# A fused attention-and-gating kernel: another order of the work inside a step, the spatial weight transposed later, and the last two batches finished together

## The chip, the cores and the metric

The kernel runs on one core of a Trainium2 chip. The metric is the device time of one launch in microseconds (us). The core's engines are TensorE (PE in the profile, its weight loads PEld), VectorE (DVE), ScalarE (ACT) and GpSimd (POOL); SyncE (SP) and POOL issue the DMAs. Each engine takes its instructions in the order of its own list, and a semaphore makes it wait for another engine where data or a buffer is still missing.

## The reference

Two layers in a row. The first is linear attention with learned features, for 8 batches, 8 heads, 576 tokens, head size 64 and 128 features:

```python
def phi(x):
    proj = np.einsum('bhsd,df->bhsf', x, w_phi)
    proj = proj - np.max(np.abs(proj), axis=-1, keepdims=True)
    return np.concatenate([np.exp(proj), np.exp(-proj)], axis=-1)
q_p, k_p = (phi(q), phi(k))
kv = np.einsum('bhsf,bhsd->bhfd', k_p, v)
z = np.sum(k_p, axis=2)
num = np.einsum('bhsf,bhfd->bhsd', q_p, kv)
den = np.einsum('bhsf,bhf->bhs', q_p, z)[..., None] + 1e-06
x = num / den                          # then heads side by side: 576 tokens x 512
```

The second is a gated layer in which tokens are mixed by a 576 x 576 matrix:

```python
h = np.maximum(x @ w_in, 0.0)          # 512 -> 1024
u, v = h[..., :512], h[..., 512:]
v_n = (v - mean(v)) / sqrt(var(v) + 1e-06)
v_s = np.einsum('ts,bsd->btd', w_spatial, v_n) + b_spatial[None, :, None]
out = (u * v_s) @ w_out                # 512 -> 512
```

## The kernel before

A batch has 576 tokens, which is four blocks of 128 and a rest of 64, called the tail. Tails of two neighbouring batches share one 128-row tile, and the two batches make a group: four groups of two batches.

**Stage A, attention, runs in steps over 36 units.** A unit is a pair of heads of one batch (four units a batch, its 512 tokens of the four blocks) or the tail of a group (all eight heads, two batches' tails). Each unit passes through a pipeline of five steps. In step `i` the kernel does, for unit `i`, the key projection (`a_keys`: matmuls L233, maxima on DVE L245, exponentials on ACT L248), the scaling of the values by the key maxima (`a_scale`: ACT L260, POOL L265 to L277), the query projection and its maxima (`a_queries`: L233, L254) and the split of the query maxima into two bfloat16 parts (`a_split`: L284 and L285). For unit `i+1` it transposes k and q (`a_transpose`, L224, copies to `kT` on ACT L227 and to `qT` on DVE L228); from batch 3 on the DMA engines deliver the transposed data, issued on SP. For unit `i-1` it transposes the maxima (`a_max_t`, L289, L290). For unit `i-2` it sums keys times values (`a_kv`, L330 and L332, copy to `kv` on ACT L334) and makes the query features (`a_qfeat`, L300 and L304, exponentials on ACT L317). For unit `i-3` it multiplies the two and divides (`a_num`, L349, L339, L340), and for unit `i-4` it transposes the quotient into `xT` (`a_x_t`, L358, L359). The order in which these parts are written inside `step` (L557) is the order in which every engine meets them.

**Stage B, the gated layer, is a queue of tasks.** When the last unit of a batch is in `xT`, `b_tasks` (L523) appends the batch's tasks: `b_v` (v half of the first product, L393, relu on ACT L395, statistics on DVE L396 and L397), `b_ln` (root and normalization on POOL, L403 to L410), `b_u` (u half, L446, L448), `b_s` (mixing by the transposed spatial weight `w_spT`, L467 and L468, gating on DVE L470) and `b_o` (output product L490, copy on ACT L492 into `ob`, DMA L498 on SP), and for the tail the same with the ending `_tail`. The function `fill` (L550) runs between the parts of a step: it adds a share of `RATE` to a credit and takes tasks from the queue as long as the credit covers half of the first task's cost. Four calls with a share of 0.25 each stand in a step; the credit is cut at `RATE / 2`. What is left in the queue after the last step runs at the end without stage A beside it.

**Tails.** For groups in `SPLIT` (L516), which are the first and the last, each batch does its own tail, so its mixing and its output follow its own u half. For the other groups only the second batch of the group holds the tail's tasks, and it runs the mixing and the output for both batches.

**The spatial weight** is transposed on PE (`transpose_spatial`, L192 to L202, copies on DVE L196 and L203): three of its five parts after step 4 and two after step 5. All products and transposes of the kernel use one pool of eight PSUM banks (L57). The output tile `ob` has four buffers. `EARLY = 7` (L165) makes the first seven units' splits run on DVE, later ones on POOL.

Of the kernel before, what the change touches and what calls it, by code (L numbers as in the profile page):

```python
# [16 lines left out]
def kernel(  # L17
# [22 lines left out]
    P = 128  # L40
# [123 lines left out]
    NM = 3  # L164
    EARLY = 7  # L165
    mhl, mT = [], []
# [44 lines left out]
    def a_transpose(u):  # L211
        src = st[u["b"]] if u["pair"] else gs[u["g"]]
        if "kT" in src:
            for x in ("kT", "qT"):
                u[x] = src[x][:, 4 * u["pj"]:4 * u["pj"] + 4, :] if u["pair"] else src[x]
            return
        pt = psum.tile([P, 2, 4, P], BF16, tag="bank", name="pt")
        for i, x in enumerate((src["k"], src["q"])):
            for j in range(4):
                if u["pair"]:  # L220
                    blk = x[:, 2 * u["pj"] + j // 2, (j % 2) * P:(j % 2 + 1) * P]
                else:
                    blk = x[:, 2 * j:2 * j + 2, :]
                nc.tensor.transpose(out=pt[:, i, j, :], in_=blk, identity=ident)  # L224
        u["kT"] = a1.tile([P, 4, P], BF16, tag="kT", name="kT")
        u["qT"] = a1.tile([P, 4, P], BF16, tag="qT", name="qT", bufs=4)
        nc.scalar.copy(out=u["kT"], in_=pt[:, 0])  # L227
        nc.vector.tensor_copy(out=u["qT"], in_=pt[:, 1])  # L228

# [90 lines left out]
    def a_kv(u):  # L320
# [5 lines left out]
        for hh in range(2):  # L326
            h = 2 * u["pj"] + hh
            for s in range(2):
                for c in range(NB):
# [3 lines left out]
                                 rhs=dg["vs"][:, bl, s, h, :], start=False, stop=True)  # L333
        nc.scalar.copy(out=d["kv"][:, 2 * u["pj"]:2 * u["pj"] + 2, :, :], in_=pv)  # L334

# [17 lines left out]
    def a_x_t(u):  # L353
        if u["pj"] == 0:
            st[u["b"]]["xT"] = s2.tile([P, KC, T0], BF16, tag="xT", name="xT", bufs=3)
        pt = psum.tile([P, NB, P], BF16, tag="bank", name="pt")
        for pos in range(NB):
            nc.tensor.transpose(out=pt[:, pos, :], in_=u["x"][:, pos].rearrange("p h d -> p (h d)"), identity=ident)  # L358
        nc.vector.tensor_copy(out=st[u["b"]]["xT"][:, u["pj"], :], in_=pt.rearrange("p n t -> p (n t)"))  # L359

# [147 lines left out]
    for g in range(G):  # L508
        units.append(dict(pair=False, g=g, i=len(units)))
# [3 lines left out]
    units[0], units[1] = units[1], units[0]  # L513
    units[0]["i"], units[1]["i"] = 0, 1
    NU = len(units)
    SPLIT = (0, G - 1)  # L516

    def unit(i):
        return units[i] if 0 <= i < NU else None
# [3 lines left out]
    def b_tasks(b):  # L523
# [22 lines left out]

    RATE = 3.4
    credit = [0.0]

    def fill(share):  # L550
        credit[0] = min(credit[0] + RATE * share, RATE / 2)
        while queue and credit[0] >= queue[0][0] / 2:
            cost, task = queue.pop(0)
            task()
            credit[0] -= cost

    def step(i):  # L557
# [3 lines left out]
        if u:  # L561
            a_keys(u)
            a_scale(u)
        fill(0.25)
        if z and z["pair"]:
            a_kv(z)
        if u:
            a_queries(u)
            a_split(u)
        fill(0.25)  # L570
        if n:
            a_transpose(n)
        if w:
            a_max_t(w)
        fill(0.25)
        if x and x["pair"]:
            a_x_t(x)
            if x["pj"] == NP - 1:
                g, bl = x["g"], x["b"] % 2
                alone = g in SPLIT  # L580
                if alone or bl == 1:
                    tail_x_t(g, [bl] if alone else [0, 1])
                queue.extend(b_tasks(x["b"]))
        if z:
            a_qfeat(z)
        fill(0.25)
        if y and y["pair"]:
            a_num(y)
            if y["pj"] == NP - 1:
                g, bl = y["g"], y["b"] % 2  # L590
                alone = g in SPLIT
                if alone or bl == 1:
                    tail_num(g, [bl] if alone else [0, 1])

    for i in range(NU + 4):
# [47 lines left out]
```

## Time and profile before

| what | value |
|---|---|
| runs | 315.26, 314.56, 315.25 us; median 315.25 us |
| profiled execution | 313.68 us, span 311.9 us |
| busy share of the span | PE 87%, DVE 69%, ACT 73%, POOL 59% |
| mean granted TensorE clock | 0.993 |
| DMA | 36.92 MB, mean 118 GB/s |

The span runs from the first to the last instruction; 1.78 us of the profiled execution lie around it. In the stretches of the profile a digit is a busy share in tenths, and in the tables of stretches the first number of an engine is its busy time in that stretch. In the rows of the timeline stand the start, the length (of all instructions of the row together), the engine and line, the operation, output and inputs, the count, and in brackets the idle time before it with what ended it.

### The profile page before, as it was taken

What the parts mean: (1) busy time and instruction counts of PE and PEld (TensorE: products, weight loads), DVE (VectorE), ACT (ScalarE), POOL (GpSimd) and SP (SyncE); (2) the same over time, 40 slices, a digit from 0 to 9 for tenths busy, and PEclk for the clock granted to TensorE, in tenths of its full rate; (3) what the DMA queues carried; (4) which work ended last, traced back from release to release, by engine and by line L of the source; (5) the groups of instructions that cost most, each with busy time, mean ns of one, the idle gap of its engine ahead of it and who ended that gap; (6) DMA issues with size and microseconds to landing.
All of it is one profiled execution on the core that took longest, in us unless ns stands there. A gap on an engine that the chain in (4) does not pass through costs nothing.

```text
span 311.9 us, 8157 instructions
## 1 busy us (share of the span) xinstructions
PE 270.8 (87%) x3149; PEld 184.7 (59%) x3194; DVE 214.3 (69%) x546; ACT 228.9 (73%) x523; POOL 183.6 (59%) x322
## 2 busy tenths in 40 slices
PE   0665888899999999898998979699999999969884
PEld 0354777566757767567675757467676675534331
DVE  6886899697867796498777956387788852812430
ACT  3487897799599978599896849599897667424603
POOL 9499547599238995648799456338777300260610
PEclk9999999999999999999999999999999999999979
DMA  7999997089222996994009999690000005203004
GB/s 109 235 190 243 183 224 63 2 115 201 95 101 63 196 221 84 231 183 146 3 2 167 132 217 218 227 239 24 2 3 2 0 36 220 56 0 135 17 2 151
DMA packets 66747, 36.92 MB, mean 118 GB/s; under 512 B 37330, under 2 KB 61074, under 8 KB 66708
## 3 DMA queue, kind: packets, MB, share of 16 engines
q0 software_dynamic: 27856, 13.77, 32.2%
q1 hardware_dynamic: 38852, 22.62, 30.1%
q8 instruction: 25, 0.41, 0.6%
q14 instruction: 14, 0.11, 0.1%
HBM read 32.85 MB, written 9.44 MB: 136 GB/s over the span
## 4 chain that ended last, share of the span: by engine, by line
PE 34%; ACT 19%; POOL 15%; DMA 14%; DVE 11%; issue 4%; SPq 2%; POOLq 0%; ACTq 0%
PE po L490 8%; ACT kf L248 7%; PE ps L467 6%; ACT qf L317 5%; DMA wspt<-in_moe_w_spatial_dram 4%; POOL vn L410 4%; DMA out_dram<-ob 4%; PE ps L233 3%; ACT vr L395 3%; DVE stats L396 3%; DMA kT_t<-k_tl 3%; POOL vs L265 3%; PE pv L393 2%; POOL rs L404 2%; DMA k_tl<-in_k_dram 2%
## 5 line engine op out<-in xcount | busy, mean ns | idle before, releaser
L265 POOL TENSOR_TENSOR vs<-v_f,em 128x512 bf16<-128x512 f32 x64 | 65.4, 1044 | 47.1 <-ACT em L260 46.9
L248 ACT ACTIVATE kf<-ps 128x512 bf16<-128x512 f32 x144 | 78.4, 650 | 14.4 <-DVE mk L245 14.2
L317 ACT ACTIVATE qf<-pq 128x512 bf16<-128x512 f32 x128 | 67.7, 660 | 10.0 <-PE pq L304 9.7
L245 DVE TENSOR_REDUCE mk<-ps 128x4 f32<-128x512 f32 x72 | 47.4, 675 | 4.7 <-PE ps L233 4.6
L254 DVE TENSOR_REDUCE mq<-ps 128x4 f32<-128x512 f32 x72 | 46.4, 679 | 2.4 <-PE ps L233 2.0
L492 ACT COPY ob<-po 128x512 f32<-128x512 f32 (+1 forms) x38 | 22.9, 610 | 31.0 <-issue 17.9
L396 DVE BATCH_NORM_STATS2 stats<-vr 128x6 f32<-128x512 bf16 (+1 forms) x38 | 25.6, 682 | 19.9 <-ACT vr L395 19.7
L467 PE MATMUL ps<-w_spT,vn 128*128 128x512 bf16 x115 | 33.7, 390 | 6.0 <-POOL vn L410 5.4
L470 DVE TENSOR_TENSOR uT<-ps,uT 128x512 bf16<-128x512 f32 x32 | 22.0, 687 | 22.3 <-PE ps L468 22.0
L393 PE MATMUL pv<-w_in_bf,xT 128*128 128x512 bf16 x119 | 31.4, 379 | 0.9 <-ACT vr L395 0.2
L446 PE MATMUL pu<-xT,w_in_bf 128*128 128x512 bf16 x119 | 31.0, 379 | 0.7 <-ACT qf_t L317 0.2
L490 PE MATMUL po<-w_out_bf,uT 128*128 128x512 bf16 x117 | 30.3, 379 | 0.5
L304 PE MATMUL pq<-mT,sel 128*128 128x128 bf16 x256 | 30.4, 219 | 0.0
L304 PEld LDWEIGHTS <-sel 128*128 128x128 bf16 x256 | 25.0, 98 | 5.8 <-issue 3.9
L395 ACT ACTIVATE vr<-pv 128x512 bf16<-128x512 f32 (+1 forms) x38 | 23.7, 668 | 5.6 <-PE pv L393 5.0
L330 PEld LDWEIGHTS <-kf 128*128 128x128 bf16 x512 | 23.0, 97 | 6.8 <-DVE mT L290 0.8
L340 DVE TENSOR_TENSOR x<-pn,rc 128x256 bf16<-128x256 f32 x64 | 26.4, 420 | 1.0
L349 PEld LDWEIGHTS <-qf 128*128 128x128 bf16 x512 | 19.8, 97 | 9.1 <-issue 4.4
L330 PE MATMUL pv<-vs,kf 128*128 128x66 bf16 x512 | 24.5, 194 | 0.7 <-DVE mT L290 0.6
L410 POOL TENSOR_SCALAR vn<-vr,rs 128x512 bf16<-128x512 bf16 x32 | 24.2, 766 | 0.7
L349 PE MATMUL pn<-kv,qf 128*128 128x66 bf16 x512 | 21.3, 193 | 3.6 <-ACT kv L334 3.3
L339 DVE RECIPROCAL rc<-pn 128x4 f32<-128x4 f32 (+1 forms) x76 | 12.0, 170 | 17.7 <-PE pn L349 17.4
(124 smaller groups left out, 568.7 us busy)
## 6 DMA issues: line engine op xcount, KB each, us to landing
out_dram<-ob SPq DMA_DIRECT2D x32, 256.0 KB, 2.6
v_f<-in_v_dram SPq DMA_DIRECT2D x6, 1024.0 KB, 6.6
k_bf<-in_k_dram POOLq DMA_DIRECT2D x7, 512.0 KB, 6.3
q_bf<-in_q_dram POOLq DMA_DIRECT2D x7, 512.0 KB, 8.5
v_f<-in_v_dram POOLq DMA_DIRECT2D x2, 1024.0 KB, 8.0
v_tl<-in_v_dram SPq DMA_DIRECT2D x8, 128.0 KB, 6.6
w_in_bf<-in_moe_w_in_dram POOLq DMA_DIRECT2D x1, 1024.0 KB, 12.5
out_dram<-ob SPq DMA_DIRECT2D x8, 128.0 KB, 2.3
```

Source lines behind the costliest of these rows:

```text
L245: nc.vector.tensor_reduce(out=u["mk"][:, hs], in_=pk, axis=AX.X, op=ALU.max, apply_absolute_value=True)
L248: nc.scalar.activation(out=u["kf"][:, s, hs, :], in_=pk, func=AF.Exp, bias=0.0, scale=sc)
L254: nc.vector.tensor_reduce(out=u["mq"][:, 4 * half:4 * half + 4], in_=pq, axis=AX.X, op=ALU.max, apply_absolute_value=True)
L265: nc.gpsimd.tensor_tensor(out=vs[:, s, :, 0:D], in0=st[u["b"]]["v"][:, pj * H:(pj + 1) * H, :], in1=em[:, s, :].unsqueeze(2).to_broadcast( ...
L304: nc.tensor.matmul(out=pq[:, 2 * par + x, :], lhsT=sel[:, j, :], rhs=m, start=False, stop=(x == 1))
L317: nc.scalar.activation(out=qf[:, s], in_=pq, func=AF.Exp, bias=0.0, scale=sc)
L330: nc.tensor.matmul(out=pv[:, hh, s, :], lhsT=u["kf"][:, s, 4 * hh + c, :], rhs=u["vs"][:, s, 4 * hh + c, :], start=(c == 0), stop=False)
L349: nc.tensor.matmul(out=pn[:, pos, :], lhsT=u["qf"][hh][:, s, pos, :], rhs=d["kv"][:, 2 * u["pj"] + hh, s, :], start=(s == 0), stop=(s == 1))
L393: nc.tensor.matmul(out=pv[r], lhsT=lhs(kc), rhs=w_in_bf[:, kc, HALF:DFF], start=(kc == 0), stop=(kc == KC - 1))
L410: nc.gpsimd.tensor_scalar(out=dst, in0=src, scalar1=rs[:, 0:1], scalar2=rs[:, 1:2], op0=ALU.mult, op1=ALU.add)
L467: nc.tensor.matmul(out=ps, lhsT=d["vn"][:, sp, cs], rhs=w_spT[:, sp, 0:T0], start=(sp == 0), stop=False)
L490: nc.tensor.matmul(out=po[r], lhsT=lhs(dc), rhs=w_out_bf[:, dc, :], start=(dc == 0), stop=(dc == KC - 1))
```

## The change

- The parts of a step stand in another order, given by a table. Before: keys, sums, queries, next transposes, maxima, out, features, attention. Now: keys, queries, sums, next transposes, attention, out, features, maxima. The shares of `fill` are 0.25 after keys, 0.25 after sums, 0.375 after attention and 0.125 after features. `RATE` is 3.29 where it was 3.4, and the credit is cut at 2.79 where it was 1.7.
- `transpose_spatial` no longer follows steps 4 and 5: its five parts are tasks of batch 0 in the queue, between `b_ln` and `b_u`.
- The last group is no longer in `SPLIT`: batches 6 and 7 share their tail's tasks, and the mixing and the output of batch 6 stand in the queue behind the u half of batch 7.
- k and q are transposed into a PSUM bank each, where they shared one.
- `EARLY` is 6 where it was 7, and for the first six units `kv` is copied by DVE where ACT did it.
- A branch for transposing `x` by DMA is written but switched off (`XX = 99`), and the list of units is built in another way with the same result.

```diff
-    EARLY = 7
+    EARLY = 6
...
-        pt = psum.tile([P, 2, 4, P], BF16, tag="bank", name="pt")
-        for i, x in enumerate((src["k"], src["q"])):
+        for x, copy in (("k", nc.scalar.copy), ("q", nc.vector.tensor_copy)):
+            pt = psum.tile([P, 4, P], BF16, tag="bank", name="pt")
...
-        nc.scalar.copy(out=u["kT"], in_=pt[:, 0])
-        nc.vector.tensor_copy(out=u["qT"], in_=pt[:, 1])
+            copy(out=u[x + "T"], in_=pt)
...
-        nc.scalar.copy(out=d["kv"][:, 2 * u["pj"]:2 * u["pj"] + 2, :, :], in_=pv)
+        copy = nc.vector.tensor_copy if u["i"] < EARLY else nc.scalar.copy
+        copy(out=d["kv"][:, 2 * u["pj"]:2 * u["pj"] + 2, :, :], in_=pv)
...
-    SPLIT = (0, G - 1)
+    SPLIT = (0,)
...
         ts.append((0.0, lambda: b_ln(b)))
+        if b == 0:
+            ts += [(0.3, lambda i=i: transpose_spatial(i)) for i in range(NB + 1)]
...
-    RATE = 3.4
+    ORDER = (("keys", 0.25), ("queries", 0), ("sums", 0.25), ("next", 0),
+             ("attention", 0.375), ("out", 0), ("features", 0.125), ("maxima", 0))
+    RATE = 3.29
+    CAP = 2.79
...
-        credit[0] = min(credit[0] + RATE * share, RATE / 2)
+        credit[0] = min(credit[0] + RATE * share, CAP)
...
-        if u and u["pair"] and u["b"] == 0 and u["pj"] == 3:
-            for x in range(3):
-                transpose_spatial(x)
-        if u and u["pair"] and u["b"] == 1 and u["pj"] == 0:
-            for x in range(3, NB + 1):
-                transpose_spatial(x)
```

At the start, the list of DVE around step 4 shows the copy of `kv` coming to it and the copies of the spatial weight leaving it (`kv` are the sums, `rc` and `x` the quotient, `mk` and `mq` the maxima of keys and queries, `mT` the transposed maxima). Before:

```order
L228 COPY qT<-pt 128x512
L339 RECIPROCAL rc<-pn 128x4
L340 TENSOR_TENSOR x<-pn,rc 128x4x64
L339 RECIPROCAL rc<-pn 128x4
L340 TENSOR_TENSOR x<-pn,rc 128x4x64
L245 TENSOR_REDUCE mk<-ps 128x4 x2
L254 TENSOR_REDUCE mq<-ps 128x4 x2
L290 COPY mT_122<-pt 16x128
L284 CAST mhl_124<-mq 128x8
L359 COPY xT<-pt 128x512
L285 TENSOR_TENSOR mhl_124<-mq,mhl_124 128x8
L196 COPY w_spT<-pt 128x576
```

And now the same stretch of DVE:

```order
L334 CAST kv<-pv 128x264
L339 RECIPROCAL rc<-pn 128x4
L340 TENSOR_TENSOR x<-pn,rc 128x4x64
L339 RECIPROCAL rc<-pn 128x4
L340 TENSOR_TENSOR x<-pn,rc 128x4x64
L289 COPY mT_130<-pt 16x128
L244 TENSOR_REDUCE mk<-ps 128x4 x2
L253 TENSOR_REDUCE mq<-ps 128x4 x2
L334 CAST kv<-pv 128x264
L283 CAST mhl_124<-mq 128x8
L227 COPY qT<-pt 128x512
L284 TENSOR_TENSOR mhl_124<-mq,mhl_124 128x8
```

The copy of `kv` stands directly ahead of the quotient that needs it, the transposed maxima come ahead of the next key maxima, and no copy of `w_spT` follows.

At the end, the list of ACT shows which tasks follow which, since each makes one kind of copy (`vr` is the v half, `uT` and `uTt` the u half of the blocks and of the tail, `ob` the output). Before, from the u half of batch 6 to the end:

```order
L448 ACTIVATE uT<-pu 128x512 x4
L460 ACTIVATE uTt<-pu 128x4x64
L492 COPY ob<-po 128x512 x4
L492 COPY ob<-po 64x512
L395 ACTIVATE vr<-pv 64x512
L395 ACTIVATE vr<-pv 128x512 x4
L448 ACTIVATE uT<-pu 128x512 x4
L460 ACTIVATE uTt<-pu 128x4x64
L492 COPY ob<-po 128x512 x4
L492 COPY ob<-po 64x512
```

Now, from the v half of batch 6 to the end:

```order
L400 ACTIVATE vr<-pv 128x512 x4
L453 ACTIVATE uT<-pu 128x512 x4
L400 ACTIVATE vr<-pv 128x512 x5
L453 ACTIVATE uT<-pu 128x512 x4
L465 ACTIVATE uTt<-pu 128x512
L497 COPY ob<-po 128x512 x9
```

Both batches' v and u halves come first (the joint tail's v half is one of the five), then all nine output copies; a second round through the tail's v half, u half and output is gone.

At the same place the list of PE goes from the tail's u half (`pu`) to the mixing (`ps`), whose weights are the normalized v (`vn`) of a batch. Before, with the numbers of the buffers (`vn_5771` is batch 7's, which POOL writes last):

```order
L458 LDWEIGHTS w_in_bf_105
L458 MATMUL pu_5848<-xTt_5158,w_in_bf_105 128x64
L467 LDWEIGHTS vn_5771
L467 MATMUL ps_5866<-w_spT_107,vn_5771 128x512
L467 LDWEIGHTS vn_5771
```

Now (`vn_5536` is batch 6's; batch 7's is `vn_5645`, which POOL writes after it):

```order
L463 LDWEIGHTS w_in_bf_105
L463 MATMUL pu_5723<-xTt_5595,w_in_bf_105 128x128
L472 LDWEIGHTS vn_5536
L472 MATMUL ps_5741<-w_spT_107,vn_5536 128x512
L472 LDWEIGHTS vn_5536
```

Behind batch 7's u half the mixing of batch 6 comes first, and that of batch 7 only after it.

More of the change, by code (lines that the diff above doesn't have):

```diff
@@ L164 @@
     NM = 3
-    EARLY = 7
+    EARLY = 6
+    XX = 99
     mhl, mT = [], []
@@ L355, in a_x_t @@
             st[u["b"]]["xT"] = s2.tile([P, KC, T0], BF16, tag="xT", name="xT", bufs=3)
+        dst = st[u["b"]]["xT"][:, u["pj"], :]
+        if XX <= u["i"] < NU - 4:
+            nc.sync.dma_start_transpose(out=dst.rearrange("p (n t) -> p n t", n=NB),
+                                        in_=u["x"].rearrange("p n h d -> p (n h d)"))
+            return
         pt = psum.tile([P, NB, P], BF16, tag="bank", name="pt")
@@ L512 @@
                 units.append(dict(pair=True, g=g, b=b, pj=pj, i=len(units)))
-    units[0], units[1] = units[1], units[0]
-    units[0]["i"], units[1]["i"] = 0, 1
+                if b == 0 and pj == 0:
+                    units.append(dict(pair=False, g=g, i=len(units)))
     NU = len(units)
-    SPLIT = (0, G - 1)
+    SPLIT = (0,)
     def unit(i):
```

78 lines of the change are left out of this document (38 added, 40 removed).

## Prediction

> **What bounds the kernel now.** I read the page's busy shares first, then the table of stretches, then the list of waits, then the timeline where a stretch shows idle time.
>
> ```profile
> PE 270.8 (87%) x3149; PEld 184.7 (59%) x3194; DVE 214.3 (69%) x546; ACT 228.9 (73%) x523; POOL 183.6 (59%) x322
> PE   0665888899999999898998979699999999969884
> ```
>
> ```profile
> core 0: us, PE busy (x) PEld busy (x) DVE busy (x) ACT busy (x) POOL busy (x), PEclk, DMA share, GB/s
> 0.00:10.00 10.00, 1.22 (x8) 0.69 (x8) 7.28 (x24) 3.07 (x4) 8.76 (x16) 1.00 1.02 130
> 10.00:31.60 21.60, 13.85 (x164) 11.04 (x165) 17.10 (x43) 15.38 (x38) 17.31 (x23) 1.00 1.15 224
> 31.60:55.00 23.40, 19.89 (x318) 16.62 (x316) 21.68 (x57) 20.43 (x50) 13.65 (x20) 1.00 1.00 153
> 55.00:128.00 73.00, 70.72 (x854) 49.51 (x867) 55.67 (x140) 62.76 (x149) 51.01 (x91) 1.00 0.70 123
> 128.00:136.00 8.00, 6.59 (x68) 3.72 (x68) 4.45 (x12) 6.07 (x13) 3.37 (x7) 1.00 1.29 197
> 144.00:168.00 24.00, 22.05 (x258) 15.48 (x259) 18.68 (x46) 21.60 (x53) 20.80 (x38) 1.00 0.21 28
> 184.00:200.00 16.00, 11.66 (x126) 7.94 (x129) 7.77 (x19) 9.64 (x24) 5.37 (x9) 1.00 1.18 205
> 200.00:272.00 72.00, 70.47 (x834) 47.80 (x849) 50.63 (x137) 56.87 (x129) 34.26 (x67) 1.00 0.24 71
> 272.00:278.00 6.00, 3.55 (x29) 1.76 (x28) 0.75 (x2) 2.42 (x5) 4.75 (x8) 1.00 0.01 3
> 294.00:298.00 4.00, 1.43 (x17) 0.68 (x15) 0.00 (x0) 0.83 (x2) 3.47 (x6) 0.91 0.00 0
> 298.00:302.00 4.00, 4.00 (x14) 1.50 (x13) 1.39 (x2) 0.00 (x0) 0.00 (x0) 0.66 0.01 4
> ```
>
> From 55 to 128 and from 200 to 272 us PE is busy for 97% and 98% of the time: in the middle the kernel is as long as PE's list. So only PE's idle time, and matmuls left out, can shorten it. The idle time lies in three places: the start up to 55 us, where PE works 34.96 of 55 us; three holes in the middle, 1.41 us (128 to 136), 1.95 us (144 to 168) and 4.34 us (184 to 200); and the end, 2.45 us from 272 to 278 and 2.57 us from 294 to 298. What ends those waits:
>
> ```profile
> DVE qT L228 <- ACT kT L227: 3.8, 7, 1.6
> PE pn L349 <- ACT kv L334: 3.3, 1, 3.3
> PE ps L467 <- POOL vn L410: 5.4, 7, 1.1
> ACT ob L492 <- DMA out_dram<-ob: 6.6, 2, 3.5
> PE ps L233 <- DMA kT_t<-k_tl: 2.1, 1, 2.1
> PE pt L289 <- POOL mhl L285: 0.9, 1, 0.9
> PE pq L300 <- ACT kf L248: 2.1, 5, 1.2
> ```
>
> The sum below goes against the profiled execution, 313.68 us; the runs' median, 315.25 us, lies 1.57 us above it. About 0.3%, 1 us, is what a measurement of this kernel can tell from no change.
>
> **Term 1, the start.** In step 3 the quotient's matmul stands still for 3.3 us, because the copy of the sums waits on ACT behind four exponentials of the tail's features:
>
> ```profile
> 26.84 2.20 ACT L317 ACTIVATE qf_t<-pq 128x512 bf16<-128x512 f32 x4
> 28.76 0.55 ACT L334 CAST kv<-pv 128x264 bf16<-128x264 f32 x1
> 29.37 0.66 PE L349 MATMUL pn<-kv,qf 128*128 128x66 bf16 x16 [3.30 <-ACT kv L334]
> 31.64 2.06 ACT L248 ACTIVATE kf<-ps 128x512 bf16<-128x512 f32 x4
> 45.23 1.03 DVE L284 CAST mhl<-mq 128x8 bf16<-128x8 f32 x1
> 46.31 0.95 DVE L285 TENSOR_TENSOR mhl<-mq,mhl 128x8 bf16<-128x8 f32 x1
> 54.94 2.07 ACT L248 ACTIVATE kf<-ps 128x512 bf16<-128x512 f32 x4
> ```
>
> Now DVE makes that copy, directly ahead of the quotient and with no exponential before it. DVE still has the query maxima, a copy of `qT` and a split ahead of it, so I leave 1.3 us of the wait and count a gain of 2.0 us.
>
> The next four steps take from 31.64 to 54.94 us, 23.3 us. In the stretch 31.6 to 55 ACT is busy 20.43 us and DVE 21.68 us of 23.40: these two, not PE, set the pace. The prices:
>
> ```profile
> L334 ACT CAST kv<-pv 128x264 bf16<-128x264 f32 x32 | 14.2, 444 | 5.9 <-PE pv L332 5.7
> L340 DVE TENSOR_TENSOR x<-pn,rc 128x256 bf16<-128x256 f32 x64 | 26.4, 420 | 1.0
> L387 DVE COPY xTt<-pt 128x256 bf16<-128x256 bf16 x4 | 1.1, 272 | 0.0
> L196 DVE COPY w_spT<-pt 128x576 bf16<-128x576 bf16 x4 | 1.7, 450 | 1.2 <-PE pt L194 1.2
> L203 DVE COPY w_spT<-pt 64x576 bf16<-64x576 bf16 x2 | 0.9, 450 | 0.2 <-PE pt L202 0.2
> ```
>
> ACT loses four copies of `kv` at 0.44 us, 1.8 us: 18.7 are left. DVE loses the spatial weight (1.7 and 0.9 us) and one split, 1.03 + 0.95, together 4.6 us. It gains four copies of `kv`. No row shows that copy on DVE: the 128x256 copy from bfloat16 takes 0.27 us, the 128x256 product that reads float32 0.42. I take 0.42, since the source is float32 here too: 1.7 us, so DVE has 18.8 left. Both engines then need 18.8 us where the steps took 23.4: the gain lies between 0 and 4.6 us. The two work in turns (maxima before exponentials), and in the present order they leave 1.7 us (DVE) and 3.0 us (ACT) unused, so I count half, 2.3 us. The two banks help here: `qT` no longer waits for `kT` (3.8 us in seven waits), but DVE alone gains by that.
>
> The spatial transposes now lie where PE is full: 30 transposes at 0.055 us each cost 1.7 us that idle time hid before.
>
> ```profile
> 190.23 0.22 PE pt L358 x4
> ```
>
> Their cover would have to be a hole of PE, and from 55 to 128 us there are 2.3 us of those in all. `w_spT` is needed first by the mixing, four tasks later, so nobody waits for it. Start: 2.0 + 2.3 - 1.7 = 2.6 us gained; bounds 1.7 us lost (no step faster) to 6.2 us gained (3.3 + 4.6 - 1.7).
>
> **Term 2, the middle.** The maxima's transpose moves to the end of its step, half a step further behind the split that it waits for: that 0.9 us goes. The hole at 128 us is ACT waiting for an output buffer whose DMA was issued late on SP, behind the tail's transposing loads. The fifth output of that batch now comes later in its step, the first one's DMA at about the same time: most of the 1.4 us goes. At 184 to 200 us one part, 2.1 us, is the wait for `kT_t`. Its load is issued by POOL at the same place of POOL's list, so I leave it. The other part is again the output buffer; SP now holds two output DMAs, not one, ahead of the transposing load that blocks it, so I count 2.2 us gained. Together 4.5 us.
>
> Against it stands a new cost. The query features of one step now come directly before the keys of the next, so ACT meets four exponentials of the one (2.2 us) and four of the other (2.06 us) with nothing between, while their four PSUM banks of eight stay taken, and `fill` hands over more tasks at a time. That PE already waits for ACT to free a bank is the row `pq L300 <- ACT kf`, 2.1 us in five waits. I allow 0.11 us in each of the 27 steps from 9 to 35, 3.0 us. Middle: 1.5 us gained; bounds 5.6 gained (all three holes but the load's, 1.41 + 1.95 + 4.34 - 2.1) and 4.5 lost (three times the allowance, 9.0, against the 4.5).
>
> **Term 3, the end.** Twice PE runs dry: after a batch's u half, the mixing needs `vn`, and POOL delivers it late.
>
> ```profile
> 286.84 3.63 PE L393 MATMUL pv<-w_in_bf,xT 128*128 128x512 bf16 x16
> 294.66 3.02 POOL L410 TENSOR_SCALAR vn<-vr,rs 128x512 bf16<-128x512 bf16 x4
> 264.25 1.05 PE L393 MATMUL pv<-w_in_bf,xTt 128*64 128x512 bf16 x4
> 308.73 0.47 SPq L504 DMA_DIRECT2D out_dram<-ob  x1
> ```
>
> The v half of batch 7 ends at 290.47 us, its `vn` at 297.68: 7.2 us, and only its u half, as many matmuls of the same width as the v half, 3.6 us, and the tail's stand between. In the new order batch 7's u half (3.6 us) and the whole mixing of batch 6 (20 such matmuls, 4.5 us) stand there, 8.1 us; for batch 6 the whole of batch 7's v and u halves, 7.2 us and more. So both holes close: 2.45 + 2.57 = 5.0 us.
>
> After the second hole the granted clock falls: 0.66 on average from 298 to 302 us, with PE busy all 4.00 us, which costs 4.00 x 0.34 = 1.4 us. Without the hole it should not fall. The first hole, just as long, left the clock at 1.00. [...]
>
> Joining the tails leaves out 28 matmuls, above all a v half and an output for the tail, 4 matmuls of 512 columns each. Such a set takes 1.05 us; I count one set and 0.15 us for the narrower matmuls, 1.2 us, since a tail's output and the next tail's v half use different halves of the array and may have run side by side; in full it would be 2.1 us. The last output is 128 rows in two DMAs where it was 64 rows in one: another issue, 0.5 us lost. End: 5.0 + 1.4 + 1.2 - 0.5 = 7.1 us gained; bounds 3.2 (half of the holes stays, and the clock falls again: 2.5 + 1.2 - 0.5) and 8.5 (both sets in full, the last issue hidden: 5.0 + 1.4 + 2.1).
>
> **Sum.** 313.68 - 2.6 - 1.5 - 7.1 = 302.5 us for a profiled execution; with the 1.57 us, 304.0 us.
>
> **The rivals.** *Only the end pays.* The steps of the start hang on one another (key maxima, exponentials, scaling), not on ACT and DVE as such, and the holes of the middle are loads that come no sooner. Then the start loses its 1.7 us, the middle nothing, and the time is 313.68 + 1.7 - 7.1 = 308.3, with 1.57 us 309.9 us. For it: the loads hold the DMA engines at a share of 1.00 to 1.15 up to 55 us. Against it: the 3.3 us behind `qf_t` is no load. Chance 0.19.
>
> *Slower: the banks.* PE waits at the joint of two steps until ACT has emptied a bank. The price is up to 2.06 us, the length of four exponentials, in each of 27 steps; it decides from (2.6 + 4.5 + 7.1) / 27 = 0.53 us per step on. At 0.7 us it makes 18.9 us, and 313.68 - 14.2 + 18.9 + 1.57 = 320 us. For it: ACT is busy 21.60 of 24 us from 144 to 168. Against it: from 55 to 128 PE is 97% busy while ACT has 10 us free. [...] Chance 0.10.
>
> *No change.* The steps pay back what the end gains: 0.41 us in each of the 27 more than I allow, 11.2 us. About 314.5 to 316 us. Chance 0.05.
>
> **How the numbers follow.** The forecast has a chance of 0.66; with the first rival that makes 0.85 faster, 0.05 the same, 0.10 slower. Terms at their good bounds together would give 313.68 - 6.2 - 5.6 - 8.5 + 1.57 = 295.0 us; that all three come so is unlikely, so the range begins at 299.0. Upwards it takes in the first rival and ends at 310.5, which leaves out the other two rivals and a little of the forecast's lower end.
>
> **What would show it.** End: no hole of PE over 0.5 us after the last step, clock 1.00, no wait of `ps` for `vn`. Start: the quotient's wait for `kv` under 1.5 us, the ninth unit's keys 4 us earlier, `w_spT` copied after 60 us. Middle: the waits of `ob` for its DMA mostly gone, that for `kT_t` still there. Wrong would be a PE busy for less than 95% from 55 to 128 us, with waits of `pq` or `ps` for ACT spread over all steps.

## The result and the profile after

| | kernel before | changed kernel |
|---|---|---|
| runs | 314.56 to 317.45 us, 4 runs | 302.3 to 305.0 us, 4 runs |
| median | 315.25 us | 303.37 us |
| profiled execution, span | 313.68 us, 311.9 us | 303.06 us, 301.3 us |

The ratio is 0.9616, with a 95% interval of 0.9551 to 0.9681: the changed kernel is faster by 12 us. The forecast was 304.0 us. Here and below a ratio compares the means of the fast runs alone (a run over 1.5% above the fastest of its kernel counts as slow), while medians are of all runs.

First the page of the changed kernel: PE's busy share, its slices, and the clock.

```profile
PE 267.4 (89%) x3124; PEld 186.4 (62%) x3166; DVE 216.8 (72%) x541; ACT 227.1 (75%) x515; POOL 183.2 (61%) x320
PE   0586987999999997799799997979999999999994
PEclk9999899999999999599999999999999999999999
```

The 9s now reach up to the last slice, so the end has no hole left. But there are 7s at the 16th and 17th slice that were not there before, and the clock has a 5 at the 17th slice. The stretches, with the columns of the prediction's table, say how much that is:

```profile
55.00:128.00 73.00, 68.28 (x838) 48.81 (x849) 54.85 (x135) 59.30 (x139) 49.08 (x90) 0.95 0.80 133
112.00:120.00 8.00, 6.21 (x93) 4.66 (x92) 5.55 (x14) 6.27 (x15) 6.28 (x11) 1.00 0.96 148
120.00:128.00 8.00, 5.70 (x41) 3.23 (x43) 2.58 (x4) 3.10 (x8) 2.01 (x5) 0.57 1.40 192
128.00:136.00 8.00, 7.80 (x95) 5.17 (x94) 5.09 (x13) 6.62 (x16) 4.23 (x8) 1.00 0.64 184
184.00:200.00 16.00, 13.24 (x152) 8.97 (x152) 8.68 (x20) 11.20 (x26) 9.11 (x16) 1.00 1.32 230
272.00:278.00 6.00, 6.00 (x30) 2.70 (x29) 4.18 (x10) 4.20 (x8) 5.29 (x11) 1.00 0.01 4
```

The holes of before at 128 and at 184 us have become smaller. A new one lies from 112 to 128 us: PE idle for 1.79 and 2.30 us, and a clock of 0.57 over 5.70 us of work, which by an estimate from these two numbers costs 5.70 x 0.43 = 2.5 us more (four matmuls of one shape, `ps` of L232, take 0.61 us at 120.24 us and 1.04 us at 124.19 us). Together that is 6.5 us. It pulls the first row down to 93.5% busy, below the 95% that the prediction named as a sign of being wrong, but without the other half of that sign, the waits for ACT. PE's waits name the cause:

```profile
PE ps L232 <- DMA kT_t<-k_tl: 4.0, 2, 2.0
...
PE pn L349 <- DVE kv L334: 2.0, 1, 2.0
PE ps L232 <- DMA qT_t<-q_tl: 1.9, 1, 1.9
PE pq L299 <- ACT ob L497: 1.6, 1, 1.6
...
PE pq L299 <- ACT kf L247: 0.2, 1, 0.2
```

The waits for `vn` (5.4 us) and for `mhl` (0.9 us) are gone, and that of `pq` for ACT's key features, which the allowance for bursts was about, fell from 2.1 to 0.2 us. The waits for the tails' transposing loads grew from 2.1 to 5.9 us. One of the two for `kT_t`, 2.0 us at 187 us, is the one of before; the other and that for `qT_t` are new, and they are the hole at 112 to 128 us.

Three places of the changed kernel's timeline measure how far each part of the program moved (`kv` on DVE, the ninth unit's keys, the last transposes of the attention), and one row of before stands against the third:

```profile
27.04 0.43 DVE L334 CAST kv<-pv 128x264 bf16<-128x264 f32 x1
50.86 2.07 ACT L247 ACTIVATE kf<-ps 128x512 bf16<-128x512 f32 x4
266.71 0.39 PE L390 MATMUL pt<-ident,xt 128*128 128x128 bf16 x4
```

```profile
269.87 0.23 PE L385 MATMUL pt<-ident,xt 64*128 64x64 bf16 x2
```

The ninth unit's keys come at 50.86 us where they came at 54.94: 4.1 us gained. The last transposes come at 266.71 where they came at 269.87: of the 4.1 us only 3.2 are left, so the stretch between the two is 0.9 us longer. From there to the end of the span it takes 34.6 us where it took 42.0: 7.4 us gained. The copy of `kv` on DVE takes 0.43 us, and 0.42 was taken.

What ate the middle's part is seen on POOL and SP, which issue the tail's loads:

```profile
106.59 0.79 POOL L61 DMA_DIRECT2D k_tl<-in_k_dram  x1 [0.28 <-issue]
107.41 2.05 POOL L264 TENSOR_TENSOR vs<-v_f,em 128x512 bf16<-128x512 f32 x2
109.55 0.73 POOL L61 DMA_DIRECT2D k_tl<-in_k_dram  x1
110.27 1.36 POOL L61 DMA_DIRECT2D q_tl<-in_q_dram  x2
```

```profile
115.96 1.21 SPq L61 DMA_TRANSPOSE kT_t<-k_tl  x1
117.28 1.20 SPq L61 DMA_TRANSPOSE qT_t<-q_tl  x1
120.24 0.61 PE L232 MATMUL ps<-wphi,kT_t 128*128 128x256 bf16 x4 [1.97 <-DMA kT_t<-k_tl]
```

The same issues, and PE's first use of `kT_t`, in the kernel before:

```profile
111.29 1.49 POOL L61 DMA_DIRECT2D k_tl<-in_k_dram  x2 [0.28 <-issue]
112.75 1.39 POOL L61 DMA_DIRECT2D q_tl<-in_q_dram  x2
118.33 1.22 SPq L61 DMA_TRANSPOSE kT_t<-k_tl  x1
122.48 0.60 PE L233 MATMUL ps<-wphi,kT_t 128*128 128x256 bf16 x4
```

PE comes to these keys 4.2 us earlier than before (at 118.27 us, without its wait of 1.97 us), and POOL's first issue comes 4.7 us earlier. But a scaling of values (2.05 us) now stands between the two halves of `k_tl`, where all four issues stood together. So `kT_t` is issued at 115.96 us, only 2.4 us earlier. The 2 us of the scaling are about what PE waits; no run moves the scaling alone. For `qT_t` this does not suffice: it is issued 2.4 us earlier and needed 2.1 us earlier (122.31 against 124.41 us). Its transfer took 6.9 us, from 117.28 to 124.19 us, and at most 4.8 us before; why is not shown.

### The profile page after: what moved, and what is told of

Its sections match the earlier page's. It is cut to its first block, busy times and chain, and to the rows that moved or that the text cites. A ratio compares the mean times of both kernels' runs of the same rounds, so it can differ in the third digit from the quotient of the medians.

```text
span 301.3 us, 8068 instructions
## 1 busy us (share of the span) xinstructions
PE 267.4 (89%) x3124; PEld 186.4 (62%) x3166; DVE 216.8 (72%) x541; ACT 227.1 (75%) x515; POOL 183.2 (61%) x320
## 4 chain that ended last, share of the span: by engine, by line
PE 60%; ACT 11%; DMA 11%; DVE 11%; issue 2%; POOL 2%; SPq 1%; ACTq 0%; POOLq 0%; DVEq 0%
PE po L495 9%; PE pv L398 8%; PE pu L451 8%; PE ps L232 7%; PE ps L472 6%; ACT kf L247 5%; DMA k_tl<-in_k_dram 4%; PE pv L329 4%; ACT qf L316 3%; PE pn L349 3%; PE pq L299 3%; PE pq L303 3%; DMA kT_t<-k_tl 3%; DMA qT_t<-q_tl 2%; DVE mk L244 2%
## 5 line engine op out<-in xcount | busy, mean ns | idle before, releaser
L247 ACT ACTIVATE kf<-ps 128x512 bf16<-128x512 f32 x144 | 76.0, 657 | 11.6 <-DVE mk L244 11.3
L244 DVE TENSOR_REDUCE mk<-ps 128x4 f32<-128x512 f32 x72 | 46.2, 681 | 7.6 <-PE ps L232 6.5
L497 ACT COPY ob<-po 128x512 f32<-128x512 f32 (+1 forms) x37 | 21.7, 600 | 24.7 <-PE po L495 20.8
L472 PE MATMUL ps<-w_spT,vn 128*128 128x512 bf16 x119 | 32.4, 379 | 0.5
L495 PE MATMUL po<-w_out_bf,uT 128*128 128x512 bf16 x118 | 31.6, 391 | 0.6 <-issue 0.2
L400 ACT ACTIVATE vr<-pv 128x512 bf16<-128x512 f32 (+1 forms) x37 | 22.5, 660 | 5.3 <-PE pv L398 4.7
L329 PEld LDWEIGHTS <-kf 128*128 128x128 bf16 x512 | 24.4, 100 | 2.9 <-issue 1.1
L329 PE MATMUL pv<-vs,kf 128*128 128x66 bf16 x512 | 25.6, 197 | 0.3 <-DVE xT L364 0.2
L340 DVE TENSOR_TENSOR x<-pn,rc 128x256 bf16<-128x256 f32 x64 | 25.3, 419 | 0.8
L283 POOL CAST mhl<-mq 128x8 bf16<-128x8 f32 x30 | 5.7, 191 | 28.1 <-DVE mq L253 28.0
```

Source lines behind the costliest of these rows:

```text
L244: nc.vector.tensor_reduce(out=u["mk"][:, hs], in_=pk, axis=AX.X, op=ALU.max, apply_absolute_value=True)
L247: nc.scalar.activation(out=u["kf"][:, s, hs, :], in_=pk, func=AF.Exp, bias=0.0, scale=sc)
L329: nc.tensor.matmul(out=pv[:, hh, s, :], lhsT=u["kf"][:, s, 4 * hh + c, :], rhs=u["vs"][:, s, 4 * hh + c, :], start=(c == 0), stop=False)
L472: nc.tensor.matmul(out=ps, lhsT=d["vn"][:, sp, cs], rhs=w_spT[:, sp, 0:T0], start=(sp == 0), stop=False)
L495: nc.tensor.matmul(out=po[r], lhsT=lhs(dc), rhs=w_out_bf[:, dc, :], start=(dc == 0), stop=(dc == KC - 1))
```

## The experiments

The theory: the joint tails alone bring the end's gain; the start's gain is real, but is lost again where the tails' loads come too late. The rivals: the new order brings the end's gain, the start's gain has another source than the two that were priced, the hole at 112 us is only where slack shows.

Every comparison was timed against the kernel before on the same chip. Its medians there were 314.4 us (the first four kernels), 314.73 us (the next four) and 316.66 us (the last four), so the ratios are compared; 0.01 of a ratio is 3.15 us. The last column is the start of the ninth unit's four key exponentials in the timeline (the expectations that name 51.9 us for the changed kernel mean the middle of the four; the ninth unit is the eighth pair of heads).

| kernel | median, us | ratio, 95% interval | ninth unit's keys, us |
|---|---|---|---|
| changed kernel | 303.37 | 0.9616, 0.9551 to 0.9681 | 50.86 |
| before, joint tails | 305.58 | 0.9727, 0.9687 to 0.9767 | 55.02 |
| changed, tails apart | 312.96 | 0.9934, 0.9895 to 0.9972 | 51.26 |
| changed, spatial weight early | 304.64 | 0.9681, 0.9637 to 0.9726 | 56.27 |
| changed, tails' loads early | 298.11 | 0.947, 0.9412 to 0.9527 | 51.30 |
| changed, `kv` copied on ACT | 304.89 | 0.9711, 0.9647 to 0.9774 | 49.83 |
| changed, old order | 308.14 | 0.9857, 0.9783 to 0.993 | 50.80 |
| changed, one bank for k and q | 308.25 | 0.983, 0.9774 to 0.9885 | 52.10 |
| before, joint tails, loads early | 305.84 | 0.9758, 0.9695 to 0.9821 | 55.32 |
| loads early, outputs issued by ACT | 293.79 | 0.935, 0.9284 to 0.9416 | 50.52 |
| loads early, old order | 311.93 | 0.9883, 0.9826 to 0.994 | 51.26 |
| loads early, one bank | 302.25 | 0.9563, 0.951 to 0.9616 | 52.32 |
| loads early, spatial weight early | 306.03 | 0.9706, 0.9655 to 0.9757 | 55.23 |

**Joint tails alone.** On the kernel before:

```diff
-    SPLIT = (0, G - 1)
+    SPLIT = (0,)
```

> The kernel before with one edit: the last pair's tails are joint. Theory (the joint tails alone close the two holes at the end, and nothing else of the change is needed for that): 7 us less than before, about 308 us; from the last of the attention's transposes to the end of the span 35 us in place of 42.0; no wait of the mixing's ps for vn, no fall of the clock after 290 us. Rival (the new order and the larger credit close the holes): under 3 us less, 312 us or more, and a hole of over 1 us with a wait for vn still stands at the end.

Measured 0.9727, 8.6 us less. The stretches of its last part, in the columns of before:

```profile
264.00:280.00 16.00, 15.89 (x126) 8.22 (x126) 9.59 (x28) 9.63 (x17) 8.60 (x16) 1.00 0.12 34
280.00:288.00 8.00, 7.95 (x48) 3.99 (x47) 4.10 (x6) 1.11 (x2) 3.68 (x7) 1.00 0.00 0
```

PE is full at clock 1.00. From the last transposes (268.27 us) to the end of the span (302.8) it takes 34.5 us, as in the changed kernel. This one edit closes both holes; the rival falls.

**Tails apart in the changed kernel**, the same edit undone:

```diff
-    SPLIT = (0,)
+    SPLIT = (0, G - 1)
```

> The changed kernel with one edit undone: the last pair's tails are apart again. Theory (the joint tails bring the end's gain): 7 us more than the changed kernel, about 310.5 us, with both holes and waits of ps for vn back in the last 35 us. Rival (the order and the larger credit bring it): within 2 us of the changed kernel, 303 to 305.5 us.

Measured 0.9934: 0.0318 or 10.0 us more than the changed kernel, and 2.1 us less than before. Two of its stretches at the end (PE's busy time and clock, then the DMA engines') and the longest wait ahead of the second:

```profile
276.00:280.00 4.00, 3.63 (x10) 0.60 0.00 0
...
296.00:300.00 4.00, 3.09 (x8) 0.66 0.02 4
```

```profile
295.70 0.39 PE L472 MATMUL ps<-w_spT,vn 128*128 128x512 bf16 x1 [1.10 <-POOL vn L415]
```

Both holes are back, ahead of these rows, and here the clock falls behind both, where it fell behind one in the profile of before. The fall that was not there before, from 276 to 280 us, costs 3.63 x 0.40 = 1.5 us by the same estimate.

**The spatial weight early**, at its old place in the changed kernel:

```diff
-        if b == 0:
-            ts += [(0.3, lambda i=i: transpose_spatial(i)) for i in range(NB + 1)]
...
+        if u and u["pair"] and u["b"] == 0 and u["pj"] == 3:
+            for x in range(3):
+                transpose_spatial(x)
+        if u and u["pair"] and u["b"] == 1 and u["pj"] == 0:
+            for x in range(3, NB + 1):
+                transpose_spatial(x)
```

> The changed kernel with the spatial weight transposed where it was before, after the fourth and fifth unit pairs of the start. Theory (the start is paced by DVE and ACT, and DVE's 2.6 us of copies lie on that path, while PE's 30 transposes cost 1.7 us where PE is full): the eighth unit's key features come 1.5 to 2.6 us later, the full stretch is 1.7 us shorter, and the time is the same within 1 us, 303 to 304.4 us. Rival one (DVE's copies at the start lie beside other work): the time is 1.7 us shorter, 301.7 us. Rival two (late transposes are hidden by waits that PE has anyway): 2 to 3 us longer, 305.5 to 306.5 us.

Measured 0.9681, 2.0 us more (the intervals overlap), and the ninth unit's keys 5.4 us later, more than any theory said. Its timeline on PE and ACT:

```profile
34.52 0.41 PE L193 MATMUL pt<-ident,wsp 128*128 128x128 bf16 x4 [2.00 <-DMA wsp<-in_moe_w_spatial_dram]
56.27 2.08 ACT L247 ACTIVATE kf<-ps 128x512 bf16<-128x512 f32 x4
```

With the faster first steps the old place comes before the weight has landed: PE waits 2.0 us for it. The move therefore does more than take copies off DVE. It takes a wait for a load off a path that had just become faster. And PE has a wait that the changed kernel does not have:

```profile
PE ps L472 <- POOL vn L415: 2.4, 4, 1.1
```

That speaks for the reason of rival two, whose 2 to 3 us are also the nearest to the measured time. The later start is swallowed in part by the waits for the tails' loads: near 120 us there is none left, and only the 1.9 us at 187 us remain.

**The tails' loads early**, in the changed kernel:

```diff
-    TS, TB = 1, 1
+    TS, TB = 3, 0
```

> The changed kernel with the tails of the next pair loaded two steps earlier, behind the load of the next batch (TS, TB = 3, 0 in place of 1, 1). Theory (the middle gave the start's gain back because the tails' transposing loads come too late: PE waits 4.0 and 1.9 us for kT_t and qT_t and then runs at a clock of 0.57 from 120 to 128 us): these waits go, PE stands still under 1.5 us from 112 to 128 us, and the time is 3 to 6 us shorter, 297.5 to 300.5 us. Rival (the waits are only where the middle's slack shows, and another wait takes their place): within 1 us of the changed kernel.

Measured 0.947, 4.6 us less than the changed kernel, as the theory said. Its stretches, and its one wait of over 2 us for ACT:

```profile
112.00:120.00 8.00, 7.89 (x106) 5.82 (x106) 6.50 (x17) 6.41 (x15) 5.25 (x8) 1.00 0.99 201
120.00:128.00 8.00, 7.85 (x99) 5.47 (x99) 5.41 (x13) 7.68 (x19) 6.11 (x11) 1.00 1.32 224
192.00:200.00 8.00, 5.50 (x45) 3.27 (x47) 3.02 (x7) 6.40 (x16) 1.37 (x6) 0.79 0.86 218
```

```profile
PE pq L299 <- ACT ob L497: 2.6, 1, 2.6
```

The hole at 112 to 128 us and the clock of 0.57 are gone, and nothing took their place there: the rival falls.

**`kv` copied on ACT** in the changed kernel:

```diff
-        copy = nc.vector.tensor_copy if u["i"] < EARLY else nc.scalar.copy
-        copy(out=d["kv"][:, 2 * u["pj"]:2 * u["pj"] + 2, :, :], in_=pv)
+        nc.scalar.copy(out=d["kv"][:, 2 * u["pj"]:2 * u["pj"] + 2, :, :], in_=pv)
```

> The changed kernel with the copy of the sums back on ACT for every unit. Theory (that copy waits on ACT behind the tail's four feature exponentials, and ACT and DVE in turns pace the steps up to the ninth unit): the quotient's wait for kv is back at about 3 us, the key features of the ninth unit are ready 1.0 to 2.5 us later than the 51.9 us of the changed kernel, 52.9 to 54.4; the tails' loads, later too by nothing that PE sees, swallow it, so that the time is within 1 us of the changed kernel. Rival one (the copy was beside other work): the ninth unit's features come within 0.7 us of the changed kernel's. Rival two (the start's gain is not swallowed): 1.5 to 2.5 us longer, 305 to 306 us.

The theory falls. The ninth unit's keys come no later (49.83 against 50.86 us), and the quotient waits less than with the copy on DVE. The copy on ACT and the quotient:

```profile
26.40 0.51 ACT L333 CAST kv<-pv 128x264 bf16<-128x264 f32 x1
26.96 0.66 PE L348 MATMUL pn<-kv,qf 128*128 128x66 bf16 x16 [1.72 <-ACT kv L333]
```

In the new order the quotient stands ahead of the features, so the tail's four exponentials no longer come before the copy on ACT. The time, 0.9711, is 3.0 us above the changed kernel's with intervals that overlap; its profile has the wait for `kT_t` at 6.6 us in place of 4.0. A cost of the copy itself is not shown, and neither is rival two's reason, since the start is not longer.

**The old order** in the changed kernel:

```diff
-    ORDER = (("keys", 0.25), ("queries", 0), ("sums", 0.25), ("next", 0),
-             ("attention", 0.375), ("out", 0), ("features", 0.125), ("maxima", 0))
-    RATE = 3.29
-    CAP = 2.79
+    ORDER = (("keys", 0.25), ("sums", 0), ("queries", 0.25), ("next", 0),
+             ("maxima", 0.25), ("out", 0), ("features", 0.25), ("attention", 0))
+    RATE = 3.4
+    CAP = 1.7
```

> The changed kernel with the order, the shares, the rate and the cap of before; the joint tails, the moved transposes, the copies on DVE and the two banks stay. Theory (the order brings part of the start and takes the 0.9 us wait for mhl away, and nothing at the end): the key features of the ninth unit 0.5 to 2 us later than in the changed kernel, waits of pq for ACT's key features back at about 2 us in 56 to 264 us, the end as in the changed kernel; 304 to 305.5 us. Rival one (the order's bursts cost in every step of the middle): 300 to 302 us. Rival two (the order carries the gain of the start): the ninth unit's features 4 us later and 306 us or more.

Measured 0.9857, 7.6 us more, with intervals apart. The start is not it: the ninth unit's keys come at 50.80 us, and with `kv` on DVE the quotient waits only 0.7 us even in the old order. In the middle PE waits for output buffers (ACT's copies of `ob` wait for a buffer's DMA, 6.6 us in the profile of before and 3.1 us in that of the changed kernel):

```profile
PE pt L363 <- ACT ob L497: 3.4, 1, 3.4
PE pv L398 <- ACT ob L497: 2.9, 1, 2.9
```

These are 6.3 us behind output buffers, where the changed kernel has 1.6, and the clock is 0.79 from 128 to 136 us and 0.57 from 200 to 208. But the waits for the tails' loads, 5.9 us in the changed kernel, are gone here, and the profiled execution, 307.38 us, lies only 4.3 us above that of the changed kernel: these rows do not add up to 7.6 us. The theory and rival one missed the size. Rival two has it (306 us or more), but for a reason that is not there, later keys. What the old order costs here stays open; the run of it with early loads, below, shows more.

**One bank for k and q** in the changed kernel, as before:

```diff
-        for x, copy in (("k", nc.scalar.copy), ("q", nc.vector.tensor_copy)):
-            pt = psum.tile([P, 4, P], BF16, tag="bank", name="pt")
+        pt = psum.tile([P, 2, 4, P], BF16, tag="bank", name="pt")
+        for i, x in enumerate((src["k"], src["q"])):
...
```

> The changed kernel with k and q transposed into one shared bank again. Theory (the second bank only spares DVE the wait for ACT's copy of kT, 3.8 us in seven waits before, and DVE is one of two engines that pace the start): the ninth unit's key features 0.3 to 1.5 us later, the waits of qT for kT back at 3 to 4 us in all, the time within 1 us of the changed kernel. Rival (PSUM is what PE lacks there, so one bank less is better): the ninth unit's features earlier than 51.5 us.

The ninth unit's keys come 1.2 us later (52.10 us), as the theory said. The time, 0.983, is 6.7 us more, which it did not. Its profiled execution was the fastest of its seven runs, 304.8 us against a median of 308.25, so the profile does not hold what made the others longer. Five of the six others have a lower mean clock, 0.972 to 0.976 against 0.989, which over some 270 us of PE's work is about 4 us by the same estimate; the sixth, 308.09 us, has 0.989 too.

**Joint tails and early loads on the kernel before**, both edits from above:

```diff
-    TS, TB = 1, 1
+    TS, TB = 3, 0
...
-    SPLIT = (0, G - 1)
+    SPLIT = (0,)
```

> The kernel before with two edits: the last pair's tails joint, and the tails loaded two steps earlier (TS, TB = 3, 0). Theory (in the kernel before the tails' loads came just in time, and only the faster start of the change runs into them): 0 to 2 us less than with the joint tails alone, 303.6 to 305.6 us, so that the rest of the change is worth 4 us or more where the loads come early (298.1 us), against 2.2 us where they come late (305.6 to 303.4). Rival (the early loads are worth 5 us by themselves): about 300.5 us, and the rest of the change is worth the same 2 us in both.

Measured 0.9758 against 0.9727 without the early loads: nothing gained. So the rest of the change is worth 0.0288 or 9.1 us where the loads come early, and 0.0111 or 3.5 us where they come late. The theory's reason, that the loads had come just in time, fits: with the joint tails alone PE has no wait for `kT_t` (2.1 us in the profile of the kernel before), so the early loads had none to take away. In return another wait grew, from 0.9 us to:

```profile
PE pt L289 <- POOL mhl L285: 3.8, 2, 3.3
```

**Output DMAs issued by ACT**, with the early loads in the changed kernel:

```diff
-        nc.sync.dma_start(out=dst, in_=ob)
+        eng = nc.scalar if 2 <= b < 6 else nc.sync
+        eng.dma_start(out=dst, in_=ob)
```

> The changed kernel with the early tail loads, and with the output DMAs of batches 2 to 5 issued by ACT behind its own copy, no longer by SP behind the transposing loads. Theory (the last hole of the middle, 2.65 us of PE and a clock of 0.79 behind it, is an output buffer whose DMA stands behind a transposing load on SP): the wait is gone, 2.5 to 3.5 us less than with the early loads alone, 294.6 to 295.6 us. Rival (16 issues at about 0.5 us each on an engine that is 77% busy hold back the emptying of PE's banks): 299 to 302 us, with waits of PE for ACT in 64 to 200 us.

Measured 0.935, 3.8 us less than with the early loads alone, a little more than the theory said (the ends of the two intervals just touch). Its stretch where the last hole was:

```profile
192.00:200.00 8.00, 7.58 (x94) 5.06 (x95) 6.84 (x18) 7.46 (x18) 3.09 (x7) 1.00 1.05 210
```

The hole and the fall of the clock behind it are gone, and the rival falls. At 293.79 us this is the fastest version of the study.

**Early loads and the old order:**

```diff
-    TS, TB = 1, 1
+    TS, TB = 3, 0
...
-    RATE = 3.29
-    CAP = 2.79
+    RATE = 3.4
+    CAP = 1.7
```

The table `ORDER` is the old one too.

> The changed kernel with the early tail loads, and with the order, the shares, the rate and the cap of before. Theory (the old order costs 4.7 us in the middle by its waits for output buffers and the cold clock behind them, whatever the loads do): 302 to 304 us, with waits of 2 us and more behind ACT's copies of ob. Rival (with the loads out of the way the order is worth nothing): within 1.5 us of the early loads alone, 296.6 to 299.6 us.

Measured 0.9883, 13 us above the early loads with the new order, nearly three times what the theory said. PE's waits, and the tail's loads in POOL's timeline:

```profile
PE pt L288 <- POOL mhl L284: 5.9, 2, 3.4
PE pt L363 <- ACT ob L497: 3.5, 1, 3.5
```

```profile
104.17 1.40 POOL L61 DMA_DIRECT2D k_tl<-in_k_dram  x2
105.51 1.41 POOL L61 DMA_DIRECT2D q_tl<-in_q_dram  x2
...
109.14 0.18 POOL L283 CAST mhl<-mq 128x8 bf16<-128x8 f32 x1
```

The four issues, 2.8 us, stand on POOL ahead of the split. In the old order the maxima's transpose follows within half a step, and PE waits up to 3.4 us. In the new order it stands at the step's end, and PE has no such wait with early loads. The same wait stands in the kernel before with early loads, where they gained nothing. The two rows make 6.8 us more than the 2.6 us for `ob` that the early loads alone have. The mean clock adds about 5 us by the same estimate: 0.969 over 271.1 us of PE's work, against 0.987 over 266.1 us.

**Early loads and one bank:**

```diff
-    TS, TB = 1, 1
+    TS, TB = 3, 0
...
-            pt = psum.tile([P, 4, P], BF16, tag="bank", name="pt")
+        pt = psum.tile([P, 2, 4, P], BF16, tag="bank", name="pt")
...
```

> The changed kernel with the early tail loads, and with k and q transposed into one shared bank. Theory (the second bank is worth the 1.8 us by which the ninth unit's key features come earlier, and no more; what was measured beyond that came from the tails' loads and the clock): 299.4 to 300.9 us. Rival one (the second bank is worth 4 to 5 us by itself): 302 to 303 us. Rival two (it is worth nothing): 297.5 to 298.7 us.

By the ratios, 0.9563 against 0.947, the second bank is worth 2.9 us; the ninth unit's keys come 1.0 us later. That lies between the theory and the first rival, and the intervals overlap by a little: inconclusive in size, though not nothing.

**Early loads and the spatial weight early**, the edits as above:

```diff
-    TS, TB = 1, 1
+    TS, TB = 3, 0
...
+            for x in range(3):
+                transpose_spatial(x)
...
```

> The changed kernel with the early tail loads, and with the spatial weight transposed where it was before. Theory (at the old place the faster start waits for the weight's load, which costs 5.4 us by the ninth unit, and with the tails' loads out of the way nothing swallows it; 1.7 us of PE come back where PE is full): 3 to 5 us more than with the early loads alone, 301 to 303 us. Rival (the delay is taken up again by the middle, as it was with the late loads): 1.2 us more, 299 to 299.8 us.

Measured 0.9706, 7.4 us more, against 2.0 us with the late loads: nothing swallows the delay any more. The ninth unit's keys, and one of PE's waits:

```profile
55.23 2.08 ACT L247 ACTIVATE kf<-ps 128x512 bf16<-128x512 f32 x4
```

```profile
PE ps L472 <- POOL vn L415: 4.8, 5, 1.8
```

The start gives 3.9 us. A second effect is PE's wait for `vn` in the mixing of the first two batches: 4.8 us, where the early loads alone have 0.4. With the 1.7 us of PE given back that makes 6.6 us of the 7.4. The wait has two parts. In the first batch (at 75 us) it is 1.5 us: in the queue the moved transposes stand between this batch's normalization and its mixing, and so they cover POOL. The other 3.3 us are in the second batch (at 113 us), where no transposes stand. There POOL has the issues of the early tails' loads ahead of the normalization, and with the late loads, above, this part is 0.9 us; that these issues are the cause fits, but was not tested alone.

## Why the prediction was right

**The total** was 0.6 us off, and in the profiled execution each term's stretch came near: the start with the moved transposes' later cost taken apart 4.1 us gained (4.3 forecast), the stretch from there to the last transposes 0.9 us lost (0.2 lost, by 1.5 gained in the middle and 1.7 for the transposes), the end 7.4 us gained (7.1). But inside the first two terms the working was wrong in part, and errors cancelled: that the sum of these two came out is luck.

**Term 3, the end: right.** The joint tails do it alone, by the mechanism given. The term was somewhat small: by the ratios the edit is worth 8.6 us on the kernel before and 10.0 us in the changed one, for 7.1 with an upper bound of 8.5. One cause is seen: with the tails apart a second fall of the clock costs 1.5 us by the estimate above, which the profile of before happened not to have. That a tail's output and the next tail's v half run side by side, which the term took as possible, the profile of before shows: their eight matmuls run from 285.84 to 286.91 us, 1.07 us, where a v half's four alone take 1.05 us (at 264.25 us). In the profile of the kernel with the joint tails alone, another 1.6 us lie ahead of the last transposes (268.27 against 269.87 us); the runs do not tell what they are.

**Term 1, the start: right size, wrong prices.** The step "DVE makes that copy, directly ahead of the quotient and with no exponential before it", 2.0 us, failed twice. The wait fell by 1.3 us, from 3.3 to 2.0. And the copy is not needed for that: in the new order ACT too has none of the tail's exponentials before it. Either edit alone takes about half of the wait away or more (1.7 us left with the copy on ACT, 0.7 in the old order, 2.0 with both), and undoing one of them made the ninth unit's keys no later; undoing both together was not run. What moved the keys, by undoing each alone, is the spatial weight, 3.9 to 5.4 us, and the second bank, 1.0 to 1.2 us.

**The spatial transposes' cost was priced with the wrong sign.** "The spatial transposes now lie where PE is full: 30 transposes at 0.055 us each cost 1.7 us" looked only at PE's work. Moving them back costs 2.0 us with intervals that overlap, and a clear 7.4 us where nothing swallows it. The prediction saw neither the wait for the weight's load, which the profile of before shows with 0.4 us and which grows as soon as the steps ahead get faster, nor that the moved work covers a wait for `vn` in the first batch: 0.4 us in the profile of before, 1.5 us in the new order with the transposes at their old place.

**Term 2, the middle.** The wait for `mhl` went as said, the hole at 128 us fell from 1.41 to 0.20 us and that at 184 us from 4.34 to 2.76 us, and the wait for `kT_t` in the latter stayed, as said (2.0 us). The allowance for bursts, 3.0 us, was not seen at all, and the rival of the banks, the slower side, has nothing for it: the row that it rested on fell to 0.2 us, and with one bank for k and q in place of two the time was 6.7 us longer, with early loads 2.9 us. What took the gain instead is a load that the sum does not have: that of the group before, needed near 120 us, for which PE does not wait in the profile of before. The sum says "Its load is issued by POOL at the same place of POOL's list, so I leave it" of the load at 184 us, where it holds. For the one near 120 us it does not: a scaling came between the halves, so `kT_t` is issued 2.4 us earlier while the need for it comes 4.2 us earlier, and the transfer of `qT_t` took longer. That cost 6.5 us in the profile. Loading early gained 4.6 us by the ratio, with the wait at 187 us gone too.

**The rival "only the end pays"** was wrong about the start, but its second half, that the loads come no sooner, holds: they are what limited the rest of the change to 3.5 us.

**Left open:** why most runs with one bank have a lower clock than the profiled one, and what the order is worth apart from loads, outputs and splits. Undoing single parts costs 10.0, 7.6, 6.7, 3.0 and 2.0 us (the last two with intervals that overlap that of the changed kernel), together more than twice the whole gain. So these are not shares of it: the parts depend on one another, as the runs with early loads show for the order and the spatial weight.

## What to carry to other kernels

When a change makes an early stage faster, list the loads that later stages need and ask what fixes the time of each: one whose issue stands in another engine's list moves along only as far as the work ahead of it does (here 2.4 us where the need for it came 4.2 us earlier), and can take the gain back where it is needed. Work that is moved has a price at the old place (what it waits for there, here 2.0 us for the weight's load) and a use at the new one (what it covers, here 1.5 us of the wait for `vn`), beside its own length. And a total that comes out right says little of its terms: here undoing each part alone showed the start's gain priced at the wrong edits and the spatial transposes with the wrong sign.

## What the runs showed of the hardware

In these runs the length of a hole alone did not decide whether the clock fell behind it. The stretches of the changed kernel (the first two rows) and of the kernel with outputs issued by ACT (the last two) show the same hole of PE near 26 us, 1.5 us idle from 26 to 28 us, and only one of them a fall, to 0.71:

```profile
26.00:28.00 2.00, 0.48 (x15) 1.00 1.13 217
28.00:30.00 2.00, 2.00 (x29) 0.71 1.11 207
```

```profile
26.00:28.00 2.00, 0.49 (x16) 1.00 1.13 217
28.00:30.00 2.00, 2.00 (x36) 1.00 1.12 208
```

From 120 to 128 us, 2.30 us of idle time came with a clock of 0.57, while the kernel with one bank was idle for 4.73 us there, in two waits of 1.92 and 2.81 us, and kept 1.00:

```profile
120.00:128.00 8.00, 3.27 (x32) 2.23 (x31) 2.50 (x7) 5.38 (x12) 3.37 (x5) 1.00 1.18 135
```

PE's longest single wait ahead of the fall at 120 us was 1.97 us. What separates the two cases is not shown. In these runs a hole thus cost its own length and, in some executions, a fall of the clock behind it, which by the estimates above cost 1.4 to 2.5 us.
